# A decode step of attention and an MLP on one core: w2's last rows in loads of 63, 63 and 2 partitions, and one transposition per block of keys

## The chip, the cores and the metric

The kernel runs on one core of a Trainium2 chip. The metric is the device time of one execution in microseconds; the median of three runs before the change is 406.31 us (406.25 to 406.46). Smaller is better.

## The reference

One token `x` of 1024 numbers is normalised, and two branches use the result `xn`. Everything is bf16.

```python
# xn = layernorm(x); the result is x + A(xn) + B(xn)
# A: attention of one query token over a cache: 32 query heads, 4 key/value heads,
#    65536 keys of 128 numbers each
q = (x @ wq).reshape(B, Sq, 32, 128).transpose(0, 2, 1, 3)
p = softmax(einsum("bhqd,bhkd->bhqk", q, repeat(k_cache, 8)) * 128 ** -0.5)
A = einsum("bhqk,bhkd->bhqd", p, repeat(v_cache, 8)) ... @ wo      # wo: 4096 x 1024
# B: h = gelu(layernorm(x) @ w1), its four quarters shifted along the sequence by 1 or 2
#    and padded with zeros, then
x1 = x + concat(g0, g1, g2, g3) @ w2                               # w2: 1024 x 1024
B = x1 + gelu(layernorm(x1) @ w3) @ w4                             # w3: 1024 x 3584, w4: 3584 x 1024
```

The sequence is one token long, so each shifted quarter consists of padding, and the vector that multiplies w2 is all zeros. The kernel still loads w2 and multiplies by it. The two caches are 64 MB each and make up most of the 170 MB that are read.

## The kernel before

**Memory.** All large operands pass through a ring of eight slots in SBUF, `slots_sb`, each 128 partitions of 8192 bf16 numbers (2 MB). The list `loads` gives the order in which SP issues transfers, the list `uses` the order in which they are consumed; `issue()` starts the next transfer in program order as soon as its slots are free. The order is wq (two transfers of 4 MB), w1, w2, w3 (two of 3.5 MB), then the sixteen half groups of keys (`load_k`, 4 MB each, two slots) with the values of the group before between them (`load_v`, 2 MB each), wo in four parts, and w4 at the end, its last part in pieces. All these transfers go through SP's queue; only the two small loads of x go through ACT's.

**w2.** The view `w2_v` gives partition p the eight rows 8p to 8p+7 of w2, 16 KB, in one transfer (L293, in `load`). `use_w2` multiplies the eight column blocks of the slot by the zero vector `g_bf` in 32 matmuls (L440), transposes the result, adds it to xn and takes the layer norm for w3. Because the vector is zero, which row of w2 sits in which place of the slot makes no difference to the sum.

**Attention.** The cache is worked through in 8 groups (two for each key/value head) of four blocks. A block is 8192 keys, 2 MB, in one slot. For each block `use_k` does this: VectorE transposes the slot, taken as 4096 float32 numbers a partition, in 32 x 32 squares into one of two buffers `X` (L522, four instructions of 1024 numbers each, one per quarter); TensorE multiplies `X` by the query arrangement `Yall` into a bank of PSUM (L529, 16 matmuls); VectorE takes the maximum of each row (L534). After four blocks `finish_group` works out the group's maximum, ScalarE takes the exponentials (L553), TensorE and ScalarE transpose them (L562, L565), and the four value blocks are multiplied (L575). Each quarter of `X` has its own record of who wrote and read it (`b_X[m][ix]`), and TensorE's matmuls wait for all four.

**Synchronisation.** Each engine has its own list of instructions, written out by the program. Each vector instruction counts up its engine's semaphore; a transfer counts up its slot's by 16. A wait that an earlier wait covers is left out. A wait that doesn't fit into an instruction becomes a semaphore instruction of its own.

**The end.** After the last values come wo's last part and w4, whose seven last pieces of 512 and 256 KB are issued at L317. The last matmuls on them (L440) are followed by one addition (L678) and the store of the result (L679).

Of the kernel before, what the change touches and what calls it, by code (L numbers as in the profile page):

```python
# [74 lines left out]
def _deps(q, reads, writes):  # L75
    for b in reads:
        for s, v in b.w.items():
            q.wait((s, v))
    for b in writes:
        for s, v in b.w.items():  # L80
            q.wait((s, v))
        for s, v in b.r.items():
            q.wait((s, v))


def _done(ev, reads, writes, partial=False):
    for b in reads:
        b.add_read(ev)
    for b in writes:
        if partial:  # L90
            b.add_write(ev)
        else:
            b.set_write(ev)


def _op(q, fn, reads=(), writes=(), partial=False):
    _deps(q, reads, writes)
    ev = q.op(fn, True)
    _done(ev, reads, writes, partial)
    return ev  # L100


def _grp(q, fns, reads=(), writes=(), partial=False):
    _deps(q, reads, writes)
    ev = None
    for i, fn in enumerate(fns):
        ev = q.op(fn, i == len(fns) - 1)
    _done(ev, reads, writes, partial)
    return ev
# [8 lines left out]
def _dma(q, chan, fn, reads=(), writes=(), partial=False):  # L118
    _deps(q, reads, writes)
    chan.n += 1  # L120
    ev = q.dma(fn, chan.sem, 16 * chan.n)
    _done(ev, reads, writes, partial)
    return ev
# [10 lines left out]
def bass_parallel_sum__gqa_block_cached__mixer_s_mlp__decode_kernel(  # L134
# [14 lines left out]
    P = 128  # L149
    D = A_x.shape[2]  # L150
# [5 lines left out]
    R = D // P  # L156
# [16 lines left out]
    SLOT = 8192  # L173

    with ExitStack() as es:
# [9 lines left out]
        def sem(name):  # L185
            return E(nc.semaphore(name))
# [66 lines left out]
        q_dve = _Q("dve", sem("c_dve"))  # L253
        q_act = _Q("act", sem("c_act"))
        q_pool = _Q("pool", sem("c_pool"))
        q_sp = _Q("sp", None)
        ch_x = _DmaChan(sem("d_x"))
        ch_out = _DmaChan(sem("d_out"))
        slots = [_Slot(slots_sb[:, i, :], _B("slot%d" % i), _DmaChan(sem("d_s%d" % i))) for i in range(NS)]
# [3 lines left out]
        b_X = [[_B() for _ in range(4)] for _ in range(2)]  # L263
# [18 lines left out]
        def take(n, uses):  # L282
            p0, free = room(n)
            assert free
            place[0] = p0 + n
            for i in range(n):
                taken[(p0 + i) % NS] = uses
            return p0 % NS

        def load(src, width=SLOT):  # L290
            i = take(1, 1)
            view = slots_sb[:, i, 0:width]
            _dma(q_sp, slots[i].chan, lambda e, view=view, src=src: e.dma_start(out=view, in_=src), writes=[slots[i].buf])  # L293
            return [(view, [slots[i].buf], i)]

        def load2(src, half=SLOT):
            i = take(2, 1)
            view = slots_sb[:, i:i + 2, :].rearrange("p s c -> p (s c)")[:, 0:2 * half]
            if 2 * half < 2 * SLOT:
                for k in range(2):  # L300
                    taken[i + k] = 2
            _dma(q_sp, slots[i].chan, lambda e, view=view, src=src: e.dma_start(out=view, in_=src), writes=[slots[i].buf, slots[i + 1].buf])
            bufs = [[slots[i].buf], [slots[i + 1].buf]] if half == SLOT else [[slots[i].buf, slots[i + 1].buf]] * 2
            return [(view[:, k * half:(k + 1) * half], bufs[k], i + k) for k in range(2)]
# [16 lines left out]

        wq_v = A_wq.rearrange("(p r) n -> p (r n)", p=P)
        w1_v = B_w1.rearrange("(p r) n -> p (r n)", p=P)
        w2_v = B_w2.rearrange("(p r) n -> p (r n)", p=P)
        w3_v = B_w3.rearrange("(p r) n -> p (r n)", p=P)
        w4_v = B_w4.rearrange("(p r) n -> p (r n)", p=P)

        def load_wq(j):
            return load2(wq_v[:, 2 * j * SLOT:2 * (j + 1) * SLOT])

        def load_w3(j):
            return load2(w3_v[:, 4 * j * F:4 * (j + 1) * F], 2 * F)
# [31 lines left out]
        for t_, val in ((selGT_bf, 1.0), (selTT, 1.0), (ident_bf, 0.0), (ones_f, 1.0), (neghalf, -0.5), (permWE, 1.0), (maskA, 1.0),  # L364
# [18 lines left out]
        ev = q_pool.op(lambda e: e.affine_select(out=maskA[:], in_=maskA[:], pattern=[[32, 4], [0, 8]],  # L383
                                                 compare_op=ALU.is_ge, fill=0.0, base=31, channel_multiplier=-1))
        for j in range(8):
            q_pool.wait(ev)
            ev = q_pool.op(lambda e, j=j: e.affine_select(out=dmask[:], in_=dmask[:], pattern=[[-1, 16]],
                                                          compare_op=ALU.not_equal, fill=1.0, base=-16 * j, channel_multiplier=1))
# [23 lines left out]
        X32 = X[:].bitcast(F32)  # L412
# [102 lines left out]
        def use_k(g, ch, ld):  # L515
            view, b = ld[0:2]
            n = g * NCH + ch
            h = g // GPH
            m = n % 2
            K32 = view.bitcast(F32)  # L520
            for ix in range(4):
                _op(q_dve, lambda e, ix=ix: e.transpose(out=X32[:, m, 1024 * ix:1024 * (ix + 1)], in_=K32[:, 1024 * ix:1024 * (ix + 1)]),  # L522
                    reads=b, writes=[b_X[m][ix]])
            fns = []
            for we in range(4):
                w_hi, e_ = divmod(we, 2)
                for c_mid in range(4):
                    mv = bass.AP(X[:].tensor, m * SLOT + c_mid * 128 + w_hi * 64 + e_, [[xstep, P], [512, CL], [2, 32]])
                    fns.append(lambda e, we=we, c_mid=c_mid, mv=mv: e.matmul(  # L529
                        S_ps[ch][32 * c_mid:32 * c_mid + 32, :], Yall[:, h, we, :, :].rearrange("p a g -> p (a g)"), mv,  # L530
                        start=(we == 0), stop=(we == 3), tile_position=(0, 32 * c_mid)))
            _grp(q_pe, fns, reads=b_X[m] + [b_Y], writes=[b_S[ch]])
            gm = g % 2
            _op(q_dve, lambda e: e.reduce_max(mcol[:, gm, ch:ch + 1], S_ps[ch][:, :], axis=AX.X), reads=[b_S[ch]], writes=[b_mcol[gm]], partial=ch > 0)  # L534
# [75 lines left out]
        for g in range(NG):  # L610
# [8 lines left out]
            if g > GPH and g % GPH == 1:  # L619
# [7 lines left out]
        _op(q_dve, lambda e: e.tensor_scalar(out=accr[:], in0=xr_bf[:], scalar1=ln_s[:, 1:2], scalar2=ln_s[:, 4:5], op0=ALU.add, op1=ALU.mult),  # L627
            reads=[b_xr, b_ln], writes=[b_accr])
        _op(q_dve, lambda e: e.tensor_tensor(out=accr[:], in0=accr[:], in1=xr_bf[:], op=ALU.add), reads=[b_xr, b_accr], writes=[b_accr])
        loaders = {"wq": load_wq, "w1": lambda: load(w1_v[:, 0:SLOT]), "w2": lambda: load(w2_v[:, 0:SLOT]), "w3": load_w3, "wo": load_wo, "w4": load_w4,  # L630
                   "k": load_k, "v": load_v}
        doubles = {"wq", "w3", "k"}

# [14 lines left out]
        for it in uses:  # L648
            ld = ready.pop(it)
            kind, args = it[0], it[1:]  # L650
            if kind == "wq":
                if args[0] == 3:
                    late_consts()
                    layer_norm(xn, b_xn, xn2, xn2_bf, b_xn2, 2)
                use_wq(args[0], ld)
            elif kind == "k":
                g, ch = args
                use_k(g, ch, ld)
                if ch == 0 and g > 0:
                    transpose_p(g - 1)  # L660
                if ch == NCH - 1:
                    finish_group(g)
            elif kind == "v":
                g, a = args
                if g == NG - 1 and a == 0:
                    transpose_p(g)
                use_v(g, a, ld)
                if a == NA - 1:
                    flash(g)
                    if g % GPH == GPH - 1:  # L670
                        combine(g // GPH)
            else:
                dict(w1=use_w1, w2=use_w2, w3=use_w3, wo=use_wo, w4=use_w4)[kind](*args, ld)
            for i in ([ld[2]] if it[0] != "w3" else [ld[2] // 2 * 2, ld[2] // 2 * 2 + 1]):
                taken[i] -= 1
            issue()
# [38 lines left out]
```

## Time and profile before

| | |
|---|---|
| median of three runs | 406.31 us |
| the profiled execution | 406.29 us |
| its span, from the first instruction to the last | 404.6 us |
| moved by DMA | 170.13 MB, 421 GB/s on average |
| busy: PE, DVE, ACT | 42%, 50%, 16% of the span |
| transfers by SP's queue (q1) | 98.5% of the time of 16 DMA engines |
| fetches of instructions (q8 and q14) | 13 packets with 0.21 MB, 5 with 0.04 MB |
| first transposition of keys (L522), last | starts at 60.46 us, 355.5 us |

PE is TensorE's matmul part, PEld its loading of weights, DVE VectorE, ACT ScalarE, SP the engine that issues transfers. A group's line in the profile gives: line of the program, engine, operation, output and input, shape, number of instructions, then their busy time in us and the mean of one in ns, then the idle time of the engine before them and what ended it. "DMA share" is the mean busy share of the core's 16 DMA engines; it can read slightly over 1 in a short window since a packet counts where it starts. A queue's line gives its packets, its megabytes and the share of the 16 engines' time; each transfer also ends with one small packet on each DMA engine that took part.

### The profile page before, as it was taken

What the parts mean: (1) busy time and instruction counts of PE and PEld (TensorE: products, weight loads), DVE (VectorE), ACT (ScalarE), POOL (GpSimd) and SP (SyncE); (2) the same over time, 40 slices, a digit from 0 to 9 for tenths busy, and PEclk for the clock granted to TensorE, in tenths of its full rate; (3) what the DMA queues carried; (4) which work ended last, traced back from release to release, by engine and by line L of the source; (5) the groups of instructions that cost most, each with busy time, mean ns of one, the idle gap of its engine ahead of it and who ended that gap; (6) DMA issues with size and microseconds to landing.
All of it is one profiled execution on the core that took longest, in us unless ns stands there. A gap on an engine that the chain in (4) does not pass through costs nothing.

```text
span 404.6 us, 4047 instructions
## 1 busy us (share of the span) xinstructions
PE 170.8 (42%) x1651; PEld 75.4 (19%) x1651; DVE 200.4 (50%) x304; ACT 65.2 (16%) x91; POOL 7.5 (2%) x38
## 2 busy tenths in 40 slices
PE   0273231223555345435335363535252436355626
PEld 0122110102212112211121131212121122122313
DVE  0255027667667665755173737571545655740010
ACT  1000000006007105200610041106010232034000
POOL 5000000000000000000000000000000000000000
PEclk9985655555655965665556655656565657655656
DMA  8999999999999999999999999999999999999995
GB/s 357 421 415 426 452 415 444 413 437 420 462 400 431 429 447 411 441 414 444 411 450 410 437 424 441 415 427 439 423 433 434 423 434 424 420 434 420 444 405 197
DMA packets 9682, 170.13 MB, mean 421 GB/s; under 512 B 1208, under 2 KB 1216, under 8 KB 2112
## 3 DMA queue, kind: packets, MB, share of 16 engines
q1 hardware_dynamic: 9512, 169.88, 98.5%
q8 instruction: 13, 0.21, 0.2%
q14 instruction: 5, 0.04, 0.0%
q10 hardware_dynamic: 152, 0.00, 0.0%
HBM read 169.87 MB, written 0.00 MB: 420 GB/s over the span
## 4 chain that ended last, share of the span: by engine, by line
DMA 57%; DVE 21%; PE 13%; issue 6%; ACT 2%; SPq 0%; POOL 0%; ACTq 0%
DMA slots_sb<-in_A_k_cache_dram 47%; DVE X L522 17%; PE S_ps L529 8%; DMA slots_sb<-in_B_w_dram 7%; DMA xr_bf<-in_A_x_dram 3%; DVE mcol L534 3%; PE OT_ps L575 2%; PE S_ps L440 2%; ACT p_sb L553 1%; ACT pT_sb L565 1%; PE PT_ps L562 1%; PE M_ps L424 0%; PE M_ps L416 0%; PE M_ps L543 0%; SPq L317 0%
## 5 line engine op out<-in xcount | busy, mean ns | idle before, releaser
L522 DVE STREAM_TRANSPOSE X<-slots_sb 128x1024 f32<-128x1024 f32 x128 | 147.7, 1211 | 39.1 <-DMA slots_sb<-in_A_k_cache_dram 39.1
L529 PE MATMUL S_ps<-X,Yall 128*32 128x512 bf16 x512 | 59.9, 614 | 150.4 <-DVE X L522 150.4
L553 ACT ACTIVATE p_sb<-S_ps,brun 128x512 bf16<-128x512 f32 x32 | 45.2, 1412 | 195.5 <-DVE brun L545 105.2
L575 PE MATMUL OT_ps<-slots_sb,pT_sb 128*32 128x512 bf16 x512 | 55.9, 584 | 12.8 <-ACT pT_sb L565 9.6
L534 DVE TENSOR_REDUCE mcol<-S_ps 128x1 f32<-128x512 f32 x32 | 22.1, 692 | 69.2 <-PE S_ps L529 69.2
L529 PEld LDWEIGHTS S_ps<-X,Yall 128*32 128x32 bf16 x512 | 17.3, 126 | 185.8 <-DVE X L522 169.4
L575 PEld LDWEIGHTS OT_ps<-slots_sb,pT_sb 128*32 128x32 bf16 x512 | 18.5, 132 | 37.9 <-issue 32.2
L565 ACT ACTIVATE pT_sb<-PT_ps 128x1024 bf16<-128x1024 bf16 x16 | 16.4, 1023 | 55.6 <-PE PT_ps L562 55.6
L562 PE MATMUL PT_ps<-ident_bf,p_sb 128*128 128x128 bf16 x128 | 15.3, 294 | 11.8 <-ACT pT_sb L565 8.9
L440 PE MATMUL S_ps<-slots_sb,xn_bf 128*32 128x512 bf16 (+1 forms) x128 | 12.6, 567 | 10.7 <-DMA slots_sb<-in_B_w_dram 9.2
L562 PEld LDWEIGHTS PT_ps<-ident_bf,p_sb 128*128 128x128 bf16 x128 | 11.4, 133 | 20.3 <-ACT pT_sb L565 11.0
L592 DVE TENSOR_TENSOR O_acc<-O_acc,OT_ps 128x512 f32<-128x512 f32 x4 | 2.8, 688 | 16.5 <-PE OT_ps L575 16.5
L440 PE MATMUL M_ps<-slots_sb,gh_bf 128*32 128x256 bf16 x112 | 6.5, 399 | 7.7 <-DMA slots_sb<-in_B_w_dram 7.6
L444 DVE STREAM_TRANSPOSE X<-S_ps 128x512 f32<-128x512 f32 (+1 forms) x3 | 2.5, 848 | 14.2 <-PE S_ps L440 14.2
L452 ACT ACTIVATE ge_a<-ge_b 128x8 f32<-128x8 f32 (+1 forms) x2 | 0.4, 217 | 52.2 <-DVE ge_b L451 52.2
L678 DVE TENSOR_TENSOR fin<-accr,M_ps 128x256 bf16<-128x256 f32 x1 | 0.4, 421 | 16.3 <-PE M_ps L440 16.3
L553 ACT ACTIVATION_READ_ACCUMULATOR p_sb<-S_ps,brun 128x1 f32 x32 | 8.5, 264 | 0.0
L440 PE MATMUL M_ps<-slots_sb,oP_bf 128*32 128x256 bf16 x128 | 7.7, 420 | 1.4 <-DVE oP_bf L604 1.4
L597 PE MATMUL M_ps<-O_acc,selX 128*128 128x128 f32 x32 | 8.2, 439 | 0.0
L440 PEld LDWEIGHTS S_ps<-slots_sb,xn_bf 128*32 128x32 bf16 x128 | 4.3, 133 | 17.0 <-DMA slots_sb<-in_B_w_dram 9.9
L597 PEld LDWEIGHTS M_ps<-O_acc,selX 128*128 128x128 f32 x32 | 7.3, 333 | 0.0
L395 DVE CAST xP<-xP_bf 128x8 f32<-128x8 bf16 x1 | 0.2, 172 | 14.2 <-DMA xr_bf<-in_A_x_dram 14.2
(97 smaller groups left out, 70.1 us busy)
## 6 DMA issues: line engine op xcount, KB each, us to landing
slots_sb<-in_A_k_cache_dram SPq DMA_DIRECT2D x16, 4096.0 KB, 26.9
slots_sb<-in_A_v_cache_dram SPq DMA_DIRECT2D x32, 2048.0 KB, 30.7
slots_sb<-in_A_wq_dram SPq DMA_DIRECT2D x2, 4096.0 KB, 16.8
slots_sb<-in_A_wo_dram SPq DMA_DIRECT2D x4, 2048.0 KB, 27.5
slots_sb<-in_B_w_dram SPq DMA_DIRECT2D x2, 3584.0 KB, 33.5
slots_sb<-in_B_w_dram SPq DMA_DIRECT2D x2, 2048.0 KB, 28.1
slots_sb<-in_B_w_dram SPq DMA_DIRECT2D x1, 4096.0 KB, 31.9
slots_sb<-in_B_w_dram SPq DMA_DIRECT2D x5, 512.0 KB, 32.4
```

Of the source, the lines that this page charges most:

```text
L440: e.matmul(out_fn(j), st_fn(kk), mv_fn(kk, j), start=st, stop=sp, tile_position=(0, 32 * j), skip_group_check=True))
L444: _op(q_dve, lambda e: e.transpose(out=X32[:, 1, c0:c0 + 32 * n], in_=src), reads=b_src, writes=[b_X[1][0]], partial=c0 > 0)
L452: _op(q_act, lambda e: e.activation(a_, bb_, ACTF.Tanh, scale=math.sqrt(2.0 / math.pi)), reads=[b_ge], writes=[b_ge])
L522: _op(q_dve, lambda e, ix=ix: e.transpose(out=X32[:, m, 1024 * ix:1024 * (ix + 1)], in_=K32[:, 1024 * ix:1024 * (ix + 1)]), reads=b, write ...
L529: fns.append(lambda e, we=we, c_mid=c_mid, mv=mv: e.matmul(S_ps[ch][32 * c_mid:32 * c_mid + 32, :], Yall[:, h, we, :, :].rearrange("p a g ...
L534: _op(q_dve, lambda e: e.reduce_max(mcol[:, gm, ch:ch + 1], S_ps[ch][:, :], axis=AX.X), reads=[b_S[ch]], writes=[b_mcol[gm]], partial=ch > 0)
L553: _op(q_act, lambda e, ch=ch: e.activation(p_sb[:, :, :, ch], S_ps[ch][:, :].rearrange("p (c i) -> p c i", i=32), ACTF.Exp, bias=brun[:, k ...
L562: _grp(q_pe, [lambda e, i=i, c=8 * c8 + i: e.transpose(out=PT_ps[:, i * P:(i + 1) * P], in_=p_sb[:, c, :, :].rearrange("p i h -> p (i h)") ...
L565: _op(q_act, lambda e, c8=c8, m=m: e.activation(pT_sb[:, m, :, 32 * c8:32 * c8 + 32, :].rearrange("p a x g -> p x a g"), PT_ps[:, :].rearr ...
L575: fns.append(lambda e, cl=cl, q4=q4: e.matmul(OT_ps[32 * q4:32 * q4 + 32, :], pT_sb[:, m, a, 4 * cl:4 * cl + 4, :].rearrange("p x g -> p ( ...
L592: _op(q_dve, lambda e: e.tensor_tensor(out=O_acc[:, :], in0=O_acc[:, :], in1=OT_ps[:, :], op=ALU.add), reads=[b_OT], writes=[b_O])
L597: fns.append(lambda e, t=t: e.matmul(M0_ps[:, 256:384], selX[:, t, :, :].rearrange("p g x -> p (g x)"), O_acc[:, t * P:(t + 1) * P], start ...
```

## The change

The first part touches w2's load. The slot now receives rows 0 to 895 of w2 as seven rows a partition (14 KB), and the last 128 rows, one a partition, in three more transfers of 63, 63 and 2 rows of 2 KB. All four transfers count up the same slot's semaphore, and the consumer waits for all of them.

The second part replaces the four transpositions of a block's quarters by one instruction over all 4096 numbers of a partition. It marks all four quarters of `X` as written at once.

```diff
-        w2_v = B_w2.rearrange("(p r) n -> p (r n)", p=P)
+        w2_v = B_w2[0:(R - 1) * P, :].rearrange("(p r) n -> p (r n)", p=P)
...
+        def load_w2():
+            view, b, i = load(w2_v, (R - 1) * D)[0]
+            sl = slots[i]
+            for p0, n in ((0, 63), (63, 63), (126, 2)):
+                ev = _dma(q_sp, sl.chan, lambda e, p0=p0, n=n: e.dma_start(out=sl.view[p0:p0 + n, (R - 1) * D:R * D], in_=B_w2[(R - 1) * P + p0:(R - 1) * P + p0 + n, :]))
+            sl.buf.set_write(ev)
+            return [(sl.view, b, i)]
...
-            for ix in range(4):
-                _op(q_dve, lambda e, ix=ix: e.transpose(out=X32[:, m, 1024 * ix:1024 * (ix + 1)], in_=K32[:, 1024 * ix:1024 * (ix + 1)]),
-                    reads=b, writes=[b_X[m][ix]])
+            _op(q_dve, lambda e: e.transpose(out=X32[:, m, :], in_=K32), reads=b, writes=b_X[m])
...
-        loaders = {"wq": load_wq, "w1": lambda: load(w1_v[:, 0:SLOT]), "w2": lambda: load(w2_v[:, 0:SLOT]), "w3": load_w3, "wo": load_wo, "w4": load_w4,
+        loaders = {"wq": load_wq, "w1": lambda: load(w1_v[:, 0:SLOT]), "w2": load_w2, "w3": load_w3, "wo": load_wo, "w4": load_w4,
                    "k": load_k, "v": load_v}
```

## The prediction

> **What bounds the kernel now.** I read the page's shares first, then its DMA queues, then the stretches at the end, then single packets.
>
> ```profile
> span 404.6 us, 4047 instructions
> PE 170.8 (42%) x1651; PEld 75.4 (19%) x1651; DVE 200.4 (50%) x304; ACT 65.2 (16%) x91; POOL 7.5 (2%) x38
> DMA  8999999999999999999999999999999999999995
> ...
> q1 hardware_dynamic: 9512, 169.88, 98.5%
> q8 instruction: 13, 0.21, 0.2%
> q14 instruction: 5, 0.04, 0.0%
> q10 hardware_dynamic: 152, 0.00, 0.0%
> ```
>
> No compute engine is over 50%, while SP's loads (q1) fill 98.5% of sixteen DMA engines' time. The kernel is a 170 MB stream with work hung beside it. The chain agrees: 57% of it is DMA, and its last long link is a 256 KB piece of w4 that was issued by 373.81 and landed 27.82 us later (start, duration, what):
>
> ```profile
> 373.81 27.82 DMA slots_sb<-in_B_w_dram
> 401.64 0.04 issue
> 401.68 0.32 PE M_ps L440 x4
> 402.00 0.02 issue
> 402.03 0.42 DVE fin L678
> ```
>
> At 421 GB/s that is a queue of nearly 12 MB, so an earlier issue of a load buys nothing: its turn comes later anyway.
>
> What is left is how the stream ends. The columns are PE, PEld, DVE, ACT, POOL, clock, DMA share, GB/s:
>
> ```profile
> 397.00:398.00 1.00, 1.00 (x24) 0.78 (x20) 0.00 (x0) 0.00 (x0) 0.00 (x0) 0.50 0.99 383
> 398.00:399.00 1.00, 0.91 (x20) 0.32 (x8) 0.00 (x0) 0.00 (x0) 0.00 (x0) 0.50 0.68 254
> 399.00:400.00 1.00, 0.61 (x8) 0.14 (x8) 0.00 (x0) 0.00 (x0) 0.00 (x0) 0.52 0.46 170
> 400.00:401.00 1.00, 0.40 (x8) 0.12 (x8) 0.00 (x0) 0.00 (x0) 0.00 (x0) 1.00 0.36 133
> 401.00:402.00 1.00, 0.59 (x8) 0.21 (x8) 0.00 (x0) 0.00 (x0) 0.00 (x0) 1.00 0.02 6
> ```
>
> The DMA share does not fall from 1 to 0 at once: 0.36 of 16 is six engines still at work after 400, with the others done. The four last rows hold 0.68 + 0.46 + 0.36 + 0.02 = 1.52 us of all engines, so an even finish would come at 399.5 instead of 401.6. That 2.1 us (0.5% of the time) is all that balancing the engines can bring.
>
> Why are six late? The records of single packets have no engine number, but a packet starts 3 or 4 ns ahead of its predecessor's recorded end on the same engine, so they can be strung into sixteen chains (a few ties stay open). In the chains every engine moves 16 KB in 611 ns (median) without a gap; what sets them apart is the fetching of instructions. Each of the 13 q8 fetches (16 KB) costs one engine about 1.5 us: 1.06 for itself, the rest in the next data packet. They go to eight engines in turn, the ninth to the first again, so five engines have two. Of the five q14 fetches (8 KB, about 0.65 to 1.0 us each), three (at 36.1, 181.4 and 348.8 us) fall on one further engine. Ends of data by chain: the five with two q8 fetches at 400.84, 400.89, 401.02, 401.16 and 401.21, the one with three q14 at 400.82, the rest between 397.8 and 399.7. The last landing, which PE waits for, is at 401.64, 0.43 after the last data.
>
> **The change part by part.** *One transposition for four (L522).*
>
> ```profile
> L522 DVE STREAM_TRANSPOSE X<-slots_sb 128x1024 f32<-128x1024 f32 x128 | 147.7, 1211 | 39.1 <-DMA slots_sb<-in_A_k_cache_dram 39.1
> L534 DVE TENSOR_REDUCE mcol<-S_ps 128x1 f32<-128x512 f32 x32 | 22.1, 692 | 69.2 <-PE S_ps L529 69.2
> ...
> 82.41 4.61 DVE L522 STREAM_TRANSPOSE X<-slots_sb 128x1024 f32<-128x1024 f32 x4
> ```
>
> The four instructions of a block take 4.61 us, overlapping a little. For one of 4096 elements the bounds are four recorded durations end to end, 4.84, and the slope between the transpositions of 512 (714 ns, L444, from PSUM) and 1024 elements: 0.97 ns an element, so 1211 + 3072 x 0.97 = 4.19. I take 4.4, since 1024 elements from SBUF are its like: VectorE saves 32 x 0.2 = 7 us (bounds: 13 saved, 7 lost). On the path I cost that at nothing: a K and a V block (4 MB) take the stream 9.9 us and VectorE about 7.3. If VectorE were the bound, the 7 us would be the gain. PE waits for all four quarters today, so no wait grows; the slot is freed about 0.2 us sooner and its reload queues behind 27 us of others.
> [...]
>
> What does reach the end is the count of instructions. PE's 3302 on 13 fetches of 16 KB make 254 a fetch, about 64 bytes each; an 8 KB fetch holds some 127. VectorE had 62, 187 and 319 behind it (semaphore instructions counted) at 36.1, 181.4 and 348.8 us: those three q14 fetches are its own. It has 347 in all; 96 fewer leave 251, so the third fetch goes and its engine ends near 399.84 instead of 400.82. PE also waits for one VectorE event a block, not four: 2 of its semaphore instructions go in 25 blocks and 1 in the 7 that begin a later group, 57 in all. The 13th q8 fetch comes 54 instructions before PE's end, so it goes too, or comes after the loads. Its engine (401.21) falls by about 1.5. The latest is then the one at 401.16: by itself this part gives -0.05 us, since four others are as late; the bounds are 0 and -0.1.
>
> *The last row of w2.* Today w2 is 128 rows of 16 KB, 8 an engine. It becomes 128 rows of 14 KB and 128 rows of 2 KB in three loads. The three issues cost SP under 0.7 us each (L293 and L302 issue in 0.33 to 0.71) at a point where it then waits 19.5 us for wq's slots: nothing. w3, k and v queue behind them with 12 MB ahead. w2 lands up to 0.6 us later; it landed at 32.49 and PE began on it at 33.60, after waiting for VectorE: covered, by 0.5 us, and past that the layer norm of x1 has 2.4 us before w3's data.
>
> How many engines take 63 rows no row shows. The two loads of x on q10 bound it: 152 packets are 128 + 4 of data and 16 + 4 that signal the end, so 128 rows go to sixteen engines and 4 rows to four, each an equal number. Equal parts of 63 on at most sixteen are 1, 3, 7 or 9. I take 9, the largest, as in both rows: 2 x 7 rows on each of nine, and the 2 rows on two. Rows of 2 KB took 84 ns (w4's last pieces). So nine engines pay 14 x 84 ns = 1.18 and save 16 KB, 0.61: +0.57 (two of them +0.65). The other seven save 0.61.
> [...]
>
> Are the late ones among the seven? The four-row load marks four chains: one is VectorE's, a second has another q14 fetch, the other two are open to ties. So the eight q8 engines look like the other half, and at least seven of them would be relieved. Then the latest ends at 401.16 - 0.61 = 400.55 instead of 401.21, VectorE's at 399.84 + 0.57 = 400.41, the early ones under 400.3: -0.66 us.
>
> **Sum.** The profiled execution took 406.29, its span 404.6 and 1.7 around it; the median of the runs is 406.31. 406.31 - 0.05 - 0.61 = 405.65.
>
> **Rivals.** *A late engine gets the rows.* The ninth may be one of those with two fetches. Its 400.84 to 401.16 becomes 401.41 to 401.73: +0.2 to +0.5; and if two engines that write the same partitions at once hold each other up, the 14 rows cost twice: another 1.2, up to +1.7. It decides as soon as one loaded engine stood less than 0.57 before the last. For it: five of the eight q8 engines are late. Against: only one of the eight need be among the nine.
> *Nothing moves.* Writes into the partitions of the seven hold them up for what they saved: 0 to -0.1. [...]
> *Better balance.* If the fetches that go were also those that delay the rest, up to the even finish: -0.8 to -2.1. Against: four engines keep two fetches.
> *Few engines.* On 3, each has 42 rows, 3.5 - 0.6 = +2.9, from which an early engine's 3.2 us of room takes all and a late one's nothing; on 1, +10, less that room: up to 416.3. Against: both rows of x.
>
> **How the numbers follow.** The forecast (-0.66, its own range 405.4 to 406.0) 0.40; better balance 0.24; nothing 0.14; a late engine 0.18, over 0.81 us in two thirds of it; few engines 0.04. Within 0.2% (0.81 us), about what a measurement of this kernel tells from no change, lie the forecast, the nothing and 0.06 of the late engine: 0.60. Faster 0.24, slower 0.12 + 0.04 = 0.16. Range 405.2 to 407.6: it drops the far half of the better balance (0.12), the few engines (0.04) and the late engine's far end (0.04).
>
> **What would show it.** q1 with 9512 + 148 = 9660 packets if nine engines take 63 rows (128 + 20 more), 9644 if one; q8 at 12 and q14 at 4; L522 x32 near 4.4 us; DMA share still 1 until 398, then a shorter tail, with the last landing near 401.0. Wrong would be: a tail as long with the same six engines, a DMA share below 0.98 in any 40 us of the middle, or w2's matmuls later than 33.6.

## The result: slower by 0.23%, and the profile after

The median is 407.35 us (406.37 to 407.85, 13 runs) beside 406.27 us (406.12 to 406.50, 13 runs) for the kernel before on the same chip: a ratio of 1.0023, with a 95% interval of 1.0014 to 1.0031. That is 1.08 us in the wrong direction. The times after are in two groups, 3 of them at 406.37 to 406.71 and 10 at 407.14 to 407.85; those of before show no such split. The profiled execution after took 407.44 us, in the upper group.

The head of the profile after and its queues, as before:

```profile
span 405.7 us, 3897 instructions
PE 173.0 (43%) x1651; PEld 74.3 (18%) x1651; DVE 194.6 (48%) x208; ACT 65.3 (16%) x91; POOL 7.5 (2%) x38
...
DMA  9999999999999999999999999999999999999994
...
q1 hardware_dynamic: 9660, 169.88, 98.5%
q8 instruction: 13, 0.21, 0.2%
...
q14 instruction: 5, 0.03, 0.0%
```

The stream is as full as before (98.5%, and nine tenths or more in every slice but the last), and q1's 9660 packets are the number that the prediction gave for nine engines taking each load of 63 rows. VectorE's 8 KB fetch is gone from q14 (four of that size are left; the fifth packet is small), but q8 still has 13. So the kernel still ends with its stream. The chain's end is the same three steps as before, 1.14 us later:

```profile
373.94 28.84 DMA slots_sb<-in_B_w_dram
402.78 0.04 issue
402.83 0.32 PE M_ps L448 x4
```

Stretches of 1 us at the end (columns as in the prediction):

```profile
397.00:398.00 1.00, 1.00 (x28) 0.76 (x20) 0.00 (x0) 0.00 (x0) 0.00 (x0) 0.50 1.01 401
398.00:399.00 1.00, 1.00 (x24) 0.51 (x16) 0.00 (x0) 0.00 (x0) 0.00 (x0) 0.50 0.98 381
399.00:400.00 1.00, 0.69 (x12) 0.14 (x8) 0.00 (x0) 0.00 (x0) 0.00 (x0) 0.65 0.72 281
400.00:401.00 1.00, 0.37 (x8) 0.12 (x8) 0.00 (x0) 0.00 (x0) 0.00 (x0) 1.00 0.46 166
401.00:402.00 1.00, 0.33 (x8) 0.10 (x4) 0.00 (x0) 0.00 (x0) 0.00 (x0) 1.00 0.14 39
402.00:403.00 1.00, 0.17 (x4) 0.10 (x4) 0.00 (x0) 0.00 (x0) 0.00 (x0) 1.00 0.01 2
```

Two things are new in the DMA share (next to last column). It holds 0.98 between 398 and 399, where it was 0.68: all engines are late, not a few. The shares from 396 on (1.03 in the row before these) add up to 4.35 us, so an even finish would now come at 400.35; the same sum for the kernel before gives 399.57. And the last stretch of the tail belongs to one engine: 0.14 of 16 is two engines, the next to last landing of the last piece is at 401.92, and a single one runs on to 402.78. **So about 0.8 us is lost by the average engine, and about 0.35 more by the last engine beyond the average.** The experiments take these two apart.

The transposition is what was forecast, and w2 is not quite:

```profile
L529 DVE STREAM_TRANSPOSE X<-slots_sb 128x4096 f32<-128x4096 f32 x32 | 142.0, 4438 | 43.9 <-DMA slots_sb<-in_A_k_cache_dram 43.9
```

```profile
34.04 1.90 PE L448 MATMUL M_ps<-slots_sb,g_bf 128*32 128x256 bf16 x32 [2.91 <-DMA slots_sb<-in_B_w_dram]
```

The second line is from the timeline: PE now waits for w2's data and begins on it at 34.04, not 33.60.

### The profile page after: what moved, and what is told of

It reads as the page before. It is cut to its first block, busy times and chain, and to the rows that moved or that the text cites. A ratio compares the mean times of both kernels' runs of the same rounds, so it can differ in the third digit from the quotient of the medians.

```text
span 405.7 us, 3897 instructions
## 1 busy us (share of the span) xinstructions
PE 173.0 (43%) x1651; PEld 74.3 (18%) x1651; DVE 194.6 (48%) x208; ACT 65.3 (16%) x91; POOL 7.5 (2%) x38
## 3 DMA queue, kind: packets, MB, share of 16 engines
q1 hardware_dynamic: 9660, 169.88, 98.5%
## 4 chain that ended last, share of the span: by engine, by line
DMA 58%; DVE 24%; PE 14%; ACT 2%; issue 1%; SPq 0%; POOL 0%; ACTq 0%
DMA slots_sb<-in_A_k_cache_dram 48%; DVE X L529 21%; PE S_ps L535 8%; DMA slots_sb<-in_B_w_dram 7%; DMA xr_bf<-in_A_x_dram 3%; DVE mcol L540 3%; PE OT_ps L581 2%; PE S_ps L448 2%; PE PT_ps L568 1%; ACT pT_sb L571 1%; ACT p_sb L559 1%; PE M_ps L448 1%; PE M_ps L432 0%; PE M_ps L424 0%; PE M_ps L549 0%
## 5 line engine op out<-in xcount | busy, mean ns | idle before, releaser
L529 DVE STREAM_TRANSPOSE X<-slots_sb 128x4096 f32<-128x4096 f32 x32 | 142.0, 4438 | 43.9 <-DMA slots_sb<-in_A_k_cache_dram 43.9
L581 PE MATMUL OT_ps<-slots_sb,pT_sb 128*32 128x512 bf16 x512 | 57.0, 595 | 13.0 <-ACT pT_sb L571 9.6
L535 PEld LDWEIGHTS S_ps<-X,Yall 128*32 128x32 bf16 x512 | 16.1, 130 | 184.4 <-DVE X L529 164.5
L581 PEld LDWEIGHTS OT_ps<-slots_sb,pT_sb 128*32 128x32 bf16 x512 | 18.0, 133 | 39.4 <-issue 33.6
## 6 DMA issues: line engine op xcount, KB each, us to landing
slots_sb<-in_A_v_cache_dram SPq DMA_DIRECT2D x32, 2048.0 KB, 30.9
slots_sb<-in_B_w_dram SPq DMA_DIRECT2D x2, 3584.0 KB, 34.1
```

The lines of the kernel that those rows point to most:

```text
L529: _op(q_dve, lambda e: e.transpose(out=X32[:, m, :], in_=K32), reads=b, writes=b_X[m])
L535: fns.append(lambda e, we=we, c_mid=c_mid, mv=mv: e.matmul(S_ps[ch][32 * c_mid:32 * c_mid + 32, :], Yall[:, h, we, :, :].rearrange("p a g ...
L581: fns.append(lambda e, cl=cl, q4=q4: e.matmul(OT_ps[32 * q4:32 * q4 + 32, :], pT_sb[:, m, a, 4 * cl:4 * cl + 4, :].rearrange("p x g -> p ( ...
```

## The experiments

The letters in the quoted expectations are short names of theories; the text after each says in words which mechanism the run speaks for. Where they speak of foreign partitions, they assume that an engine fills the same eight partitions in every load over all 128; no view numbers the engines or names a packet's partition, so this was not shown. Each kernel differs from the changed one only by the edit shown.

**1. The transposition alone.** w2's load and its view are those of before.

```diff
-        w2_v = B_w2[0:(R - 1) * P, :].rearrange("(p r) n -> p (r n)", p=P)
+        w2_v = B_w2.rearrange("(p r) n -> p (r n)", p=P)
-        loaders = {..., "w2": load_w2, ...
+        loaders = {..., "w2": lambda: load(w2_v[:, 0:SLOT]), ...
```

> One transposition per block, w2 loaded in one transfer as before. Theory A (the loads of 63 rows cost the time: nine engines get more bytes, and while they write the partitions that other engines are filling, all are held up): no slower than before, 0.0 to -0.3 us, so 406.0 to 406.3; VectorE's third fetch is gone, PE's semaphore instructions are 25 instead of 82, and the tail after 398 us has five late engines instead of six. Theory B (the long transposition or the shifted instruction fetches cost it): about +1 us, 407.2 to 407.4, with the last landing near 402.7.

Measured: 406.29 us (406.08 to 406.38, 11 runs), ratio 0.9999 (0.9990 to 1.0008). That leaves room for the forecast's -0.05 and none for the loss. Its last two landings are at 401.48 and 401.54, and the tail has the old shape, with several engines ending together:

```profile
399.00:400.00 1.00, 0.40 (x8) 0.12 (x8) 0.00 (x0) 0.00 (x0) 0.00 (x0) 1.00 0.51 188
400.00:401.00 1.00, 0.46 (x12) 0.18 (x12) 0.00 (x0) 0.00 (x0) 0.00 (x0) 1.00 0.25 94
401.00:402.00 1.00, 0.64 (x8) 0.15 (x8) 0.00 (x0) 0.00 (x0) 0.00 (x0) 0.75 0.00 0
```

**2. w2's loads alone.** The four transpositions come back.

```diff
-            _op(q_dve, lambda e: e.transpose(out=X32[:, m, :], in_=K32), reads=b, writes=b_X[m])
+            for ix in range(4):
+                _op(q_dve, lambda e, ix=ix: e.transpose(out=X32[:, m, 1024 * ix:1024 * (ix + 1)], in_=K32[:, 1024 * ix:1024 * (ix + 1)]),
+                    reads=b, writes=[b_X[m][ix]])
```

> w2's last row in loads of 63, 63 and 2, the four transpositions as before. Theory A: slower by +0.7 to +1.3 us, 407.0 to 407.6; besides the engine with the fifth and thirteenth fetch of PE's instructions, VectorE's engine, which keeps three fetches, is late too (400.8 + 1.1 = about 401.9). Theory B: 406.3, as before.

Measured: 407.55 us (407.22 to 407.58, 6 runs), ratio 1.0029 (1.0018 to 1.0041). The loads of w2 carry the whole loss. The last landing is at 402.79 here too; strung into chains, its engine is the one with VectorE's three fetches, which carries w2's small rows too, while no loaded engine has two of PE's fetches in this profile; and no run fell below 407.2. So the fetch that the long transposition saves is worth something only beside w2's loads.

**3. The 128 rows in one load.** If small rows as such were the cost, it would stay.

```diff
-            for p0, n in ((0, 63), (63, 63), (126, 2)):
+            for p0, n in ((0, 128),):
```

> [...] Theory A (uneven shares and foreign partitions): the packets of 2 KB stay near 84 ns, no slow packets of w3 behind them, and the time is that of the kernel with the transposition alone, within 0.2 us of 406.2. Theory C (small rows or the extra transfers in themselves): about 407.3.

Measured: 406.45 us (406.17 to 406.84, 11 runs), ratio 1.0003 (0.9994 to 1.0012). Rows of 2 KB cost nothing that can be measured when sixteen engines share them: w2's 128 take 84 ns at the median, the longest 92. (406.45 is 0.05 us outside the expected 406.2 within 0.2; the interval takes in no change.)

**4. Two loads of 64 rows.** q1's packets are 9672: 16 engines in each load, 4 rows each, so bytes and engines are as even as in run 3. Only the place is other, since each load covers half of the partitions.

```diff
-            for p0, n in ((0, 63), (63, 63), (126, 2)):
+            for p0, n in ((0, 64), (64, 64)):
```

> As the changed kernel, but two loads of 64 rows, four rows on each of sixteen engines: the shares are even, but in each load all engines write into one half of the partitions. If uneven shares alone cost the time: 406.2, like one load of 128 rows. If writing foreign partitions costs by itself: packets of 2 KB near 160 ns while the load runs, all sixteen engines later by about 0.6 us, 406.6 to 407.0.

Measured: 407.02 us (406.82 to 407.27, 11 runs), ratio 1.0019 (1.0010 to 1.0028), in one group. With the same bytes on every engine, more than half of the loss is there. By the assumption above, a load of 64 on sixteen engines sends some of them to partitions that are another's; what is measured is the packets. I added up the durations of all packets and divided by sixteen (us of the average engine):

| kernel | all packets | the 2 KB packets | w3's 28 KB packets |
|---|---|---|---|
| run 3, one load of 128 | 399.69 | 2.05 | 17.16 |
| run 4, 64 + 64 | 400.42 | 2.34 | 17.53 |
| changed kernel, 63 + 63 + 2 | 400.68 | 2.33 | 17.82 |
| run 5, seven engines | 400.79 | 2.34 | 17.99 |
| run 6, seven engines, steps of four | 399.67 | 1.38 (258 packets, not 384; w2's other rows are 63 of 4 KB, 0.63) | 17.18 |

A 2 KB packet of w2 takes up to 238 ns in run 4, and 64 of the changed kernel's 128 take over 110 (none in run 3). The larger part is on w3, the next load in the queue: while some engines still write w2's rows, others are already in w3, and 25 of its 256 packets take 1.2 to 1.76 us (2 in run 3; the median is 1.06). Of these 25, 23 start between 31.2 and 33.1, and w2's small rows are written from 30.9 to 33.1. A few slow packets of w3 come without such rows too (7 before, 12 in run 1, all after 33.6), for which no run names the cause. The two columns rise by 0.28 and 0.66 us from run 3 to the changed kernel, of 0.99 in all.

**5. Seven engines.** The prediction held the engines with two fetches for the other half. Loads of 49, 21 and 7 rows go to seven engines, in equal parts: q1's packets are 9670, 158 more than before, which is 128 rows and 4 x 7 + 2 at the loads' ends.

```diff
-            for p0, n in ((0, 63), (63, 63), (126, 2)):
+            for p0, n in ((0, 49), (49, 49), (98, 21), (119, 7), (126, 2)):
```

> As the changed kernel, but the 128 rows come in loads of 49, 49, 21, 7 and 2, which seven engines share (the last load two of them): 18 rows of 2 KB on each, none on the other nine. Theory D: the engines that fetch PE's instructions in turn are eight, two of which are among the nine that took the rows in the changed kernel; which of the eight begins differs from execution to execution, and the executions above 407 us are those in which one of these two has two fetches. Then here no such engine takes rows, no run is above 407.0, the median is 406.4 to 406.8, and what is over before's time is the holding up through foreign partitions, as with 64 and 64. Theory E (the load on the engines alone, whoever fetches): more rows on each than in the changed kernel, 407.5 and more.

Measured: 407.37 us (406.76 to 408.08, 8 runs), ratio 1.0027 (1.0017 to 1.0038), in two groups: four at 406.76 to 407.09, four at 407.64 to 408.08. The idea that seven loaded engines leave the fetching ones free fell: strung into chains, two of the eight that fetch for PE carry w2's small rows here as well as in the changed kernel.

**6. The same seven engines, in steps of four partitions.** The small rows go to a buffer of their own, in nine loads of seven pieces of 4 KB with steps of four partitions and one load of two rows. The steps were meant to keep each engine to the partitions that it fills in the other loads, which no view shows. The product of these 128 rows with the zero vector is left out.

```diff
+        w2x = sb("w2x", [P, 4 * D], BF)
...
-            for p0, n in ((0, 63), (63, 63), (126, 2)):
-                ev = _dma(...)
+            r0 = (R - 1) * P
+            sets = [32 * a + o for a in range(2) for o in range(4)]
+            for t, p0 in enumerate(sets + [0]):
+                c = 0 if t < 8 else 2
+                src = B_w2[r0 + 14 * t:r0 + 14 * (t + 1), :].rearrange("(a b) n -> a (b n)", b=2)
+                ev = _dma(q_sp, sl.chan, lambda e, p0=p0, c=c, src=src: e.dma_start(out=w2x[p0:p0 + 25:4, c * D:(c + 2) * D], in_=src))
+            ev = _dma(q_sp, sl.chan, lambda e: e.dma_start(out=w2x[1:6:4, 2 * D:3 * D], in_=B_w2[r0 + 126:r0 + 128, :]))
...
-            rows_mv(R, d_parts(view, 0), ...
+            rows_mv(R - 1, d_parts(view, 0), ...
```

> [...] Theory D: packets of 4 KB stay near 160 ns, none of w3's packets behind them is slow; the engines with PE's fetches end 0.6 us earlier, VectorE's engine 0.9 later (400.7), so 405.7 to 406.1, faster than before. If foreign partitions don't matter: the same time as the run with loads of 49. If late engines don't set the end: 406.3 or more.

Measured: 406.91 us (405.67 to 407.35, 12 runs), ratio 1.0006 (0.9997 to 1.0015), in two groups: five at 405.67 to 406.16, seven at 406.89 to 407.35. Their means, 405.83 and 407.05, stand 1.1 and 0.9 us below those of run 5's groups (406.92 and 407.95), and the packets' sum is that of run 3 again (399.67). So **the cost on every engine goes with the partitions that a load names, not with how many engines write**. That engines hold each other up in the same partitions is my reading of it. Run 6 also differs in the size of its pieces, in the buffer and in the product left out; runs 3 and 4 differ in none of these, and the ten loads of run 6 show that many loads are not the cost either. The expected 405.7 to 406.1 came true in the lower group alone. The profiled execution is of the lower group (405.69), with the earliest end so far:

```profile
400.00:401.00 1.00, 0.47 (x12) 0.10 (x4) 0.00 (x0) 0.00 (x0) 0.00 (x0) 1.00 0.12 45
401.00:402.00 1.00, 0.29 (x4) 0.10 (x4) 0.42 (x1) 0.00 (x0) 0.00 (x0) 1.00 0.00 0
```

**7 and 8. The changed kernel again, and 11. Run 6 again**, one execution each, for more profiles of the groups. No edit.

> The changed kernel once more, for another profiled execution. Theory D: the single packets show PE's first fetch on another engine than in the first profile, and the time is 407.1 to 407.9 if one of the two fetching engines among the nine has two fetches, 406.3 to 406.7 if both have one. If the order of the fetches is fixed: the same order, with the fifth and sixth fetch on these two.

> The changed kernel a third time, with the same expectation: the order of the fetches decides between about 407.4 and about 406.5.

> The kernel with seven engines and their own partitions once more, for a second profiled execution. Theory D2: if it is one of the slow ones (406.9 to 407.4), its last landing is that of one loaded engine with two fetches of PE's instructions, at about 402.0 to 402.6, and the others end by 401.2; if it is a fast one (405.7 to 406.2), both fetching engines among the seven have one.

Measured: 407.55, 407.38 and 406.86 us, all upper group. The last two landings of the last piece are at 401.73 and 402.79, at 401.80 and 402.64, at 401.04 and 402.10: each time one engine is alone for 0.8 to 1.1 us. In run 11 that is one engine's 0.04 of 16 in the middle row:

```profile
400.00:401.00 1.00, 0.17 (x10) 0.12 (x8) 0.00 (x0) 0.00 (x0) 0.00 (x0) 1.00 0.14 51
401.00:402.00 1.00, 0.53 (x12) 0.10 (x4) 0.00 (x0) 0.00 (x0) 0.00 (x0) 0.93 0.04 14
402.00:403.00 1.00, 0.41 (x4) 0.11 (x4) 0.40 (x1) 0.00 (x0) 0.00 (x0) 0.50 0.00 0
```

Who is it? In the chains, the changed kernel's last engine carries w2's small rows and has two of PE's fetches, at 175.6 and 400.3 us in the first profile, at 34.1 and 294.8, and at 34.0 and 301.4 in the other two, at 32.2 and 301.6 in run 5's, and at 32.3 and 300.8 in run 11's. The eight engines are served in turn, but the turn does not begin at the same one in every execution: the two loaded engines had fetches 5 and 6 of the thirteen in the first profile (5 comes again as 13), 1 and 8 in runs 5, 7, 8 and 11 (1 again as 9), and 7 and 8 in run 6's lower group, which have no second one. The durations of the fetches show the turn without chains. They repeat with a period of eight (after, 1.06, 1.10, 1.11, 1.09 and 1.02 us come again as 1.06, 1.11, 1.10, 1.09 and 1.04; before, the second is off, 0.99 beside 1.07), and in every profile two neighbours of 1.02 or 1.03 us stand between one of 1.09 and one of 1.07; where the chains name these two, they are the loaded ones. They are fetches 8 and 9 in seven of the thirteen profiles, 7 and 8 in three, 6 and 7 in one, 5 and 6 in two.

That explains the groups: low when neither loaded engine has two fetches. With thirteen fetches on eight engines in turn, two neighbours are both without a second one at two of eight starts; the low group had 12 of the 36 executions of the changed kernel and runs 5 to 8 and 11. Five profiles of the upper group and one of the lower (run 6's) fit this; of the changed kernel's and run 5's lower groups there is no profile, so for them it is argued.

**9 and 10. Fewer engines, in steps of four partitions.** Half of the 128 rows in one load over all partitions, the other half in loads of five or of two pieces, for five or two engines. "Lowest" in the expectations is my name for the engines that the smallest loads take. The product with zeros is left out and the buffer `w2x` added as in run 6.

```diff
+            ev = _dma(q_sp, sl.chan, lambda e: e.dma_start(out=sl.view[:, (R - 1) * D:(R - 1) * D + 512], in_=B_w2[r0:r0 + 64, :].rearrange("r (h n) -> (r h) n", h=2)))
# run 9: seven loads, five engines
+            for t, p0 in enumerate((0, 1, 2, 3, 32, 33)):
+                src = B_w2[r0 + 64 + 10 * t:r0 + 64 + 10 * (t + 1), :].rearrange("(a b) n -> a (b n)", b=2)
+                ev = _dma(q_sp, sl.chan, lambda e, p0=p0, src=src: e.dma_start(out=w2x[p0:p0 + 17:4, 0:2 * D], in_=src))
+            ev = _dma(...: e.dma_start(out=w2x[34:39:4, 0:2 * D], in_=...))
# run 10: eight loads, two engines
+            for t, p0 in enumerate((0, 1, 2, 3, 32, 33, 34, 35)):
+                src = B_w2[r0 + 64 + 8 * t:r0 + 64 + 8 * (t + 1), :].rearrange("(a b) n -> a (b n)", b=4)
+                ev = _dma(q_sp, sl.chan, lambda e, p0=p0, src=src: e.dma_start(out=w2x[p0:p0 + 5:4, 0:4 * D], in_=src))
```

> [...] The product of the 128 rows with the zero vector is left out. Shares against before: five engines +0.8 us, eleven -0.25. Theory D2 (of the eight engines that fetch PE's instructions two are among the lowest seven, so a kernel that loads these seven has fast and slow executions): if neither of the two is among the lowest five, all executions lie at 405.8 to 406.2; if one or both are, some lie at 406.7 to 407.2 again. If the share of an engine were no matter: all at 406.3.

> As the run with five engines, but the second half goes in eight loads of two pieces of 8 KB to the two lowest engines, one of which makes one short fetch and the other none in all profiles: these two get +2.3 us, fourteen -0.25. Theory D2: no slow executions, since both had 2.2 us and more of room: 406.0 to 406.4 in every run, range under 0.5 us. If the time went with the load of the fullest engine alone: 408.5.

Measured: 405.97 us (405.86 to 406.19, 11 runs), ratio 0.9992 (0.9983 to 1.0001), and 406.01 us (405.90 to 406.16, 11 runs), ratio 0.9992 (0.9983 to 1.0000). Neither has an upper group, so with five or two loaded engines no execution put a second fetch on top of the load. Run 9's profile began the turn as those of runs 5, 7, 8 and 11 did (the two fetches of 1.02 to 1.03 us are 8 and 9) and is fast all the same: in its chains the five loaded engines are VectorE's, two with one other fetch on q14 and two with none (one tie with an unloaded engine stays open). These are the best medians of the study, some 0.3 us under the kernel before, which their intervals do not tell from no change. Run 10 also says that giving an early engine 56 KB more than before (72 KB of these rows instead of 16, some 2.3 us by its packets) does not hurt. The tail of run 9 is shorter, with the last two landings together, at 401.25 and 401.29:

```profile
399.00:400.00 1.00, 0.19 (x8) 0.00 (x0) 0.00 (x0) 0.00 (x0) 0.00 (x0) 1.00 0.46 166
400.00:401.00 1.00, 0.70 (x12) 0.22 (x12) 0.00 (x0) 0.00 (x0) 0.00 (x0) 1.00 0.21 80
401.00:402.00 1.00, 0.29 (x4) 0.10 (x4) 0.32 (x1) 0.00 (x0) 0.00 (x0) 0.97 0.00 0
```

**The two losses apart.** For each profile, the even finish (396 plus the DMA shares of the stretches from there to 404) and the last landing:

| kernel | even finish | last landing | between them |
|---|---|---|---|
| before | 399.57 | 401.64 | 2.07 |
| run 1, transposition alone | 399.44 | 401.54 | 2.10 |
| run 3, one load of 128 | 399.42 | 401.59 | 2.17 |
| run 6 (lower), run 11 (upper): seven, steps of four | 399.39, 399.36 | 401.04, 402.10 | 1.65, 2.74 |
| run 9, five, steps of four | 399.44 | 401.29 | 1.85 |
| run 10, two, steps of four | 399.38 | 401.20 | 1.82 |
| run 4, 64 + 64 | 400.12 | 402.33 | 2.21 |
| changed kernel, three profiles | 400.35, 400.26, 400.17 | 402.78, 402.79, 402.64 | 2.43, 2.53, 2.47 |
| run 2, w2 alone | 400.52 | 402.79 | 2.27 |
| run 5, seven engines | 400.57 | 402.89 | 2.32 |

The kernels that load w2's last rows over all 128 partitions, in steps of four or in both ways lie at 399.36 to 399.57, those with loads of 49, 63 or 64 neighbouring partitions at 400.12 to 400.57. From run 1 to the changed kernel's first profile the landing moves by 1.24 us: 0.91 of it is the even finish, 0.33 the last engine's lag.

## Why the prediction was wrong

It forecast 405.65 us, a gain of 0.66. The 407.35 us measured still lies in its range of 405.2 to 407.6, but only because the range made room for the rivals; the forecast had the direction wrong. What happened is nearest to the rival in which a late engine gets the rows, with the doubled price for two engines that write the same partitions; it had a chance of 0.18 and bounds of +0.2 to +1.7, and +1.08 lies among them.

**What failed: "Are the late ones among the seven?"** The step took the eight engines that fetch for PE to be "the other half", at least seven of them relieved. Two of the eight are among the loaded ones, even among the seven of run 5. The step also took the loads of 63 to use the engines of x's four-row load, which no run had shown then; that part held, since in chains of the profile after (a few ties stay open) the four engines of x's rows all carry w2's small rows. And the step treated "the late engines" as fixed ones because one trace showed one order of fetches; where the order begins differs between executions. In the kernel before, this does not matter, since the eight are alike and five of them have two fetches whichever begins. With loads on some of the eight it does, in about two of three executions (24 of 36). By itself, with the packets' sum at run 3's level (399.67 beside 399.69), this step's error is what separates run 6's two groups, 405.67 to 406.16 from 406.89 to 407.35. The lower one reaches the 405.65 forecast.

**What was mis-sized: the terms of w2's last row.** "+0.57" for nine engines and "-0.61" for seven conserve the average to within 0.05 us ((9 x 0.57 - 7 x 0.61) / 16). In the changed kernel's chains the four loaded engines without fetches ended at 399.09 to 399.50, 1.1 to 1.5 later than the engines without fetches before (397.97 in the middle), and the unloaded ones some 0.3 later (the one without fetches at 398.26) instead of 0.61 earlier. With 1.1 to 1.5 for the nine, (9 x 1.1 + 7 x 0.3) / 16 = 0.75 and (9 x 1.5 + 7 x 0.3) / 16 = 0.98, and the even finish's 0.78 lies between them. The price of 84 ns was taken from rows loaded over all 128 partitions (w4's last pieces); w2's small rows took 111 at the median and up to 201 in the profile after. The doubling stood in a rival as a possibility, at 1.2 us on the engines that take the rows and without a row behind it; it came to 0.5 to 1.0 there and reached the other engines too. The trace of before held nothing that could have shown it. The rival "nothing moves" also had the unloaded engines held up, but only by what they saved; they ended some 0.3 later. That writes into the same partitions do it, as both rivals had it, no run shows directly.

**What also failed, harmlessly or nearly.** The thirteenth q8 fetch was to go or to come after the loads. It came at 400.31, when the loads ran on past it, and on the last engine at that; in run 1, whose loads are those of before, it came at 399.6. The cover of w2's landing was thinner than thought: PE began 0.44 us later than before. No load waited for that: the DMA row of the page after has no slice below nine tenths there.

**What held.** The bound (a full stream whose last engine sets the end); the transposition at 4.4 us (4.438) off the path, and at most 0.1% in either direction for it (run 1, where -0.05 was forecast); 9660 packets; 96 VectorE instructions and 57 semaphore instructions of PE fewer (347 to 251 and 82 to 25 in the trace); VectorE's third fetch gone; the issues on SP free (runs 9 and 10 make eight and nine of them without a loss). The equal parts held in every packet count (63 rows on nine engines give 9660, 64 on sixteen 9672, 49, 21 and 7 on seven 9670). By the counts sixteen engines share the rows alike in runs 3 and 4 (406.45 and 407.02 us), so unequal shares do not make the difference between these two.

## What to carry to other kernels

Where a kernel is one full stream of loads like this one, be wary of loads of some neighbouring partitions only: those of 49, 63 and 64 cost the average engine 0.7 to 1.1 us here, the next load's packets included, while the same rows over all 128 partitions at once (run 3) or in steps of four (runs 6, 9 and 10) did not. Extra bytes can be put on engines that end early, but only if they end early in every execution: take several profiles before calling an engine early. Two numbers from the profile tell which loss one has: the sum of the DMA shares at the end (did the average engine get later?) and the last landing less that even finish (did one engine?).

## What the runs showed of the hardware that was not expected

- Packets slowed down in and after loads of 49, 63 or 64 neighbouring partitions: 2 KB ones from 84 to as much as 238 ns (run 4), and of the next load's 256 packets of 28 KB, 18 to 33 take over 1.2 us instead of the usual 1.06 (2 in run 3); for 256 KB of rows in two to five loads, 0.7 to 1.1 us of all engines (sums of packets: 400.42 to 400.79 against 399.69). That engines held each other up in the same partitions is an inference; no view shows which engine writes which partition.
- PE's 16 KB instruction fetches go to eight of the sixteen DMA engines in turn, and the one that begins differs between executions of the same program; two neighbours in that turn were among the loaded seven or nine engines in the profiles whose chains were strung. The kernel before, whose load is even over the eight, has one group of times (406.09 to 406.70 in all rounds); run 6, whose load is not, has two (405.67 to 406.16 and 406.89 to 407.35).
